# Attention with head mixing and a rational feed-forward layer: the planner spaces bulk transfers evenly during attention

## The chip, the core and the metric

The kernel runs on 1 core of a Trainium2 chip. The metric is the device time of one execution in microseconds. Three runs gave 833.57, 831.95 and 833.22 us; the median is 833.22 us.

## What is computed

The reference, cut to what matters (batch 4, 12 heads, 448 positions, head size 64; the feed-forward layer has 1792 tokens, width 768, inner width 2048):

```
scores = scale * np.matmul(q, k.transpose(0, 1, 3, 2))
scores = np.einsum('bhij,hg->bgij', scores, w_pre)
scores = scores - np.max(scores, axis=-1, keepdims=True)
attn = np.exp(scores)
attn = attn / (np.sum(attn, axis=-1, keepdims=True) + 1e-09)
attn = np.einsum('bhij,hg->bgij', attn, w_post)
x = np.matmul(attn, v)
...
h = x @ w_in
P = a[0] + a[1] * h + a[2] * h2 + a[3] * h3
Q = 1.0 + np.abs(b[0]) * np.abs(h) + np.abs(b[1]) * h2
g = P / (Q + 1e-06)
return (g @ w_out).astype(np.float32)
```

All products are of float32 accuracy; the weights come as 64-bit floats, and the chip splits each into a high and a low 32-bit part.

## The kernel before

**Attention** works on 16 tiles of query rows, four per batch element, of 120 or 88 rows. For each tile six pairs of heads are multiplied on TensorE (`put_qk`, line 482, matmul on line 496, PSUM tile `ps_s`). Each head's scores are copied to SBUF by ACT or DVE (tile `st`), and then a transfer on SP's queue, the **shuffle** (line 512, `d<-st`), lays them out so that heads lie along the partitions. There are twelve shuffles per tile, one per head. The first matmul of the next stage (`put_pre`, line 565, `ps_t` or `ps_u` from `d`) mixes the heads and waits for all twelve shuffles of its tile. A tile is worked on in groups of two blocks of ten rows: mix (L565), maximum (L571, DVE), exponential (L580, ACT), sum and reciprocal, mix again (L640, `ps_a`), transpose (L656, DVE), and, when a tile's groups are through, the product with V (L705, `put_av`, 56 matmuls in the profile for each third). The shuffles of tile T are issued while TensorE works on the groups of tile T - 1. The scores of tile 0 are made ahead of all that.

**Bulk transfers** share SP's queue with the shuffles: loads of Q (L363, 384 KB), K (L375, six parts of 224 KB per batch element from the second on), V (L679, three of 384 KB and one of 192 KB per element), weights (L405, tile `cr`), stores of the attention output (L728, `x_scr`), and, for the first two blocks of weights (`VIA = (0, 1)`), stores of the split weights to DRAM (L449, `w_scr`). Those two blocks are split by ACT, POOL and DVE in between during attention and come back at the end of it (L843).

**The feed-forward part** begins near 346 us and runs 64 units of 18 + 18 matmuls (L879, L969) with the rational function on ACT and DVE in between.

**The order of the work** on each engine is set by the class `Plan`. Every step is an operation with an engine, an assumed duration, operations that it depends on, a due time `at` and an earliest time `since`. `Plan.run` (line 73) walks through planner time: for each engine it takes, among the operations that are ready, the one with the smallest `at`. For SP it also holds `dma_free`, the assumed time at which the transfers issued so far have moved (bytes at 300 GB/s), and lets SP run ahead of it by 3.0 us at most. The result is an order per engine. On the chip each engine follows its order and waits for semaphores; no planner time is left in the program. SP, too, waits at a transfer whose data are not there, and what stands behind it waits with it.

The helper `bulk` (line 356) adds a load or store on SP; the weight loads (line 451) and the stores to `w_scr` (line 470) are added directly, as are the shuffles (line 529).

Of the kernel before, what the change touches and what calls it, by code (L numbers as in the profile page):

```python
# [37 lines left out]
CV = 384  # L38
# [5 lines left out]
class Op:  # L44
    __slots__ = ("eng", "dur", "fn", "deps", "at", "extra", "start", "end", "left", "behind", "since", "n", "on", "pick", "mode", "late")

    def __init__(self, eng, dur, fn, deps, at, extra, since, mode, late):
        self.late = late
        self.since, self.on, self.pick, self.mode = since, None, isinstance(eng, dict), mode
        self.eng, self.dur, self.fn, self.at, self.extra = eng, dur, fn, at, extra  # L50
        self.deps = deps
        self.start = self.end = None


class Plan:
# [8 lines left out]
    def __init__(self):  # L64
        self.ops = []

# [6 lines left out]
    def run(self):  # L73
# [36 lines left out]
        order = []  # L110
        last = None
        while True:
            if "sp" in free:
                free["sp"] = max(free["sp"], dma_free - self.AHEAD)
            best = None
            for e in todo:
# [4 lines left out]
                if todo[e]:  # L121
                    t = free[e]
                elif wait[e]:
                    t = max(free[e], wait[e][0][0])
                else:
                    continue
# [5 lines left out]
            while wait[e] and wait[e][0][0] <= t:  # L132
                _, n, op = heapq.heappop(wait[e])
                if op.on:
                    continue
                heapq.heappush(todo[e], (op.at, n, op))
            op = todo[e][0][2]
            if e == "pe" and op.mode != last:
                more = [x for x in todo[e] if not x[2].on and x[2].mode == last and x[0] <= op.at + self.SLACK]
                if more:  # L140
                    op = min(more)[2]
# [100 lines left out]
def mixed_attention_then_rational_ffn(ctx: ExitStack, tc, q, k, v, w, wmix, mask, a, b2, out):  # L242
# [113 lines left out]
    def bulk(dur, fn, deps, at, nbytes, **more):  # L356

        return add("sp", dur, fn, deps, at=at, extra=dma(nbytes), **more)

# [39 lines left out]
    def put_w(f, c, at, since=0.0, g=None):  # L399
# [50 lines left out]

        ld = add("sp", 0.45, load, [R["cr"].take()], at=at - 5.0, extra=dma(128 * CV * 8), since=max(since, at - 9.0))
        near = lambda i, k: [] if g is None else [posts[min(g + i, len(groups) - 1)][k]]
# [16 lines left out]
        if f in VIA:  # L469
            o8 = add("sp", 0.57, store, [o7], at=at, extra=dma(128 * CV * 8), late=2.0)  # L470
            R["co"].uses[-1].append(o8)
# [583 lines left out]
    for u in range(len(units)):  # L1055
# [3 lines left out]
        put_unit(u)  # L1059

    with tc.manual_schedule():
        for op in plan.run():
# [59 lines left out]
```

## Time and profile before

| what | value |
|---|---|
| median of 3 runs | 833.22 us (831.95 to 833.57) |
| profiled execution, its own time | 835.32 us |
| its span, first to last instruction | 833.5 us |
| mean granted TensorE clock | 0.994 of full speed |
| busy: PE, DVE, ACT, POOL | 804.6, 698.1, 503.1, 217.4 us |

Busy time is the time in which an engine has an instruction under way; the rest of the span it waits. PE is TensorE, SP the engine that issues most transfers. The profiled execution lies 2.1 us above the median of the runs.

### The profile page before, as it was taken

Reading aid. Unit: us, or ns where it says so; the run is one execution under the profiler, and the core shown is the slowest. Engines: PE = TensorE matmul, PEld = TensorE weight load, DVE = VectorE, ACT = ScalarE, POOL = GpSimd, SP = SyncE. Lnnn points to the kernel's source line nnn. Section 1 sums busy time; section 2 is a strip of 40 time slices with the busy share of each in tenths; the row PEclk is TensorE's granted clock in tenths of the full one; section 3 lists DMA queues with packets and bytes.
Section 4 is the critical chain, followed back from the end, with each engine's and each line's share of the span. In section 5 each row is a group of like instructions: output and inputs, shape, how many; then the busy total and the mean of one; then the engine's idle time right before and its main releaser. Section 6 shows DMA issues by size and latency. Waiting matters only on the chain.

```text
span 833.5 us, 23249 instructions
## 1 busy us (share of the span) xinstructions
PE 804.6 (97%) x9360; PEld 598.0 (72%) x9360; DVE 698.1 (84%) x1262; ACT 503.1 (60%) x1094; POOL 217.4 (26%) x388
## 2 busy tenths in 40 slices
PE   6899999998999899999999999999999999999997
PEld 1244445554455455588999999999999999999997
DVE  5677778787887878898999999999889999877775
ACT  2456656655564556567776676676666676745632
POOL 2224434342442334612211112122222222200000
PEclk9999999999999999999999999999999999999999
DMA  6676788678766855965731364664476635466314
GB/s 207 214 218 201 209 267 275 187 213 274 231 189 199 260 176 170 328 189 209 255 124 61 101 240 117 212 142 85 102 231 179 166 91 107 90 226 232 124 53 155
DMA packets 69724, 152.31 MB, mean 183 GB/s; under 512 B 12432, under 2 KB 50160, under 8 KB 68464
## 3 DMA queue, kind: packets, MB, share of 16 engines
q1 hardware_dynamic: 65560, 138.84, 51.0%
q0 software_dynamic: 3456, 11.01, 8.3%
q8 instruction: 74, 1.21, 0.6%
q10 hardware_dynamic: 600, 0.97, 0.4%
q14 instruction: 34, 0.28, 0.1%
HBM read 75.92 MB, written 36.18 MB: 134 GB/s over the span
## 4 chain that ended last, share of the span: by engine, by line
PE 60%; DVE 3%; ACT 1%; DMA 1%; issue 1%; POOL 0%; ACTq 0%; POOLq 0%
PE ps_s L879 27%; PE ps_u L969 9%; PE ps_a L969 9%; PE ps_t L969 9%; PE ps_a L640 2%; PE ps_s L496 1%; PE ps_u L705 1%; PE ps_t L565 1%; PE ps_u L565 1%; DMA w<-w_scr 1%; PE ps_t L705 0%; ACT e L580 0%; DVE cg L424 0%; DVE nm L571 0%; DVE cm L430 0%
## 5 line engine op out<-in xcount | busy, mean ns | idle before, releaser
L656 DVE STREAM_TRANSPOSE aa<-ps_a 128x448 f32<-128x448 f32 (+1 forms) x184 | 107.5, 617 | 12.7 <-PE ps_a L640 12.1
L879 PE MATMUL ps_s<-xs,w 128*128 128x448 f32 x504 | 107.5, 366 | 0.2 <-DVE m L908 0.2
L879 PE MATMUL ps_s<-d,w 128*128 128x448 f32 x504 | 107.6, 367 | 0.0
L496 PE MATMUL ps_s<-kk,q 64*64 64x448 f32 x720 | 94.8, 553 | 8.3 <-DMA kk<-in_k 5.1
L236 ACT COPY st<-ps_s 120x448 f32<-120x448 f32 (+1 forms) x116 | 58.2, 533 | 71.5 <-PE ps_s L496 34.2
L446 POOL TENSOR_TENSOR w<-cm,w 128x384 fp32r<-128x384 f32 x48 | 56.2, 1171 | 171.6 <-ACT w L236 133.7
L879 PEld LDWEIGHTS ps_s<-xs,w 128*128 128x128 f32 x504 | 94.4, 188 | 8.9 <-DVE m L908 0.6
L879 PEld LDWEIGHTS ps_s<-d,w 128*128 128x128 f32 x504 | 94.3, 188 | 8.9 <-issue 0.5
L640 PEld LDWEIGHTS ps_a<-e,krs 64*32 64x32 f32 x2880 | 45.1, 106 | 75.4 <-issue 29.1
L600 POOL TENSOR_SCALAR krs<-kpost,rr 128x64 f32<-128x64 f32 x180 | 80.7, 462 | 70.4 <-DVE rr L591 48.8
L640 PE MATMUL ps_a<-e,krs 64*32 64x224 f32 x2880 | 94.1, 358 | 1.6 <-DVE aa L656 0.9
L892 ACT ACTIVATE m<-ps_s,a_sb 128x448 f32<-128x448 f32 x64 | 46.3, 724 | 68.9 <-PE ps_s L879 68.5
L969 PE MATMUL ps_t<-g,w 128*128 128x448 f32 x336 | 84.0, 366 | 1.2 <-ACT g L236 1.0
L969 PE MATMUL ps_a<-g,w 128*128 128x448 f32 x336 | 84.1, 366 | 0.0
L969 PE MATMUL ps_u<-g,w 128*128 128x448 f32 x336 | 83.9, 366 | 0.0
L580 ACT ACTIVATE e<-ps_t,nm 128x448 f32<-128x448 f32 x92 | 57.7, 634 | 25.5 <-DVE nm L571 21.4
L580 ACT ACTIVATE e<-ps_u,nm 128x448 f32<-128x448 f32 x88 | 55.3, 635 | 28.9 <-DVE nm L571 24.1
L969 PEld LDWEIGHTS ps_t<-g,w 128*128 128x128 f32 x336 | 63.0, 188 | 7.0 <-ACT g L236 1.2
L969 PEld LDWEIGHTS ps_u<-g,w 128*128 128x128 f32 x336 | 63.1, 188 | 5.4
L969 PEld LDWEIGHTS ps_a<-g,w 128*128 128x128 f32 x336 | 63.1, 188 | 5.4
L496 PEld LDWEIGHTS ps_s<-kk,q 64*64 64x64 f32 x720 | 29.7, 135 | 50.4 <-issue 21.5
L587 POOL TENSOR_SCALAR sm<-sm 128x2 f32<-128x2 f32 (+1 forms) x92 | 20.9, 227 | 140.1 <-ACT e L580 138.3
(90 smaller groups left out, 1468.2 us busy)
## 6 DMA issues: line engine op xcount, KB each, us to landing
d<-st SPq DMA_DIRECT2D x144, 210.0 KB
cr<-in_w SPq DMA_DIRECT2D x64, 384.0 KB
d<-x_scr SPq DMA_DIRECT2D x5, 2688.0 KB
xs<-x_scr SPq DMA_DIRECT2D x4, 2688.0 KB
o_scr<-o POOLq DMA_DIRECT2D x24, 448.0 KB, 6.0
d<-st SPq DMA_DIRECT2D x42, 157.5 KB
x_scr<-xs SPq DMA_DIRECT2D x12, 540.0 KB
q<-in_q SPq DMA_DIRECT2D x16, 384.0 KB
```

Source lines behind the costliest of these rows:

```text
L236: eng.copy(o, i)
L446: eng.tensor_sub(t[:, 1, :], box["m"].bitcast(F32), t[:, 0, :].bitcast(F32))
L496: nc.tensor.matmul(box["s"][hh][i0:i1, 0:S], lhsT=Q[T][d, pr, i0:i1], rhs=K[b][d, pr, :], start=True, stop=True)
L565: nc.tensor.matmul(box[r if nt == 2 else 0]["t"][64 * c:64 * c + 64, 0:S], lhsT=kpre[p], rhs=Dt[T][p, kb + c if nt == 2 else kb, :], start ...
L580: nc.scalar.activation(e, box[r]["t"][:, 0:S], AF.Exp, bias=box[0]["nm"][:, r:r + 1], accum_out=box[0]["sm"][:, r:r + 1])
L587: nc.gpsimd.tensor_scalar_add(sm, sm, 1e-9)
L600: eng.tensor_scalar_mul(box[r]["kr"], kpost, rr)
L640: nc.tensor.matmul(banks[c]["p"][q_:q_ + BT, JH * r:JH * (r + 1)], lhsT=box[r]["kr"][p, m_, :], rhs=box[r]["e"][p, JH * jh:JH * (jh + 1)], ...
L656: nc.vector.transpose(o, src)
L879: nc.tensor.matmul(h[:, 0:S], lhsT=W[fi][:, wi, kk * 128:(kk + 1) * 128], rhs=x[:, kk // 3, xj, kk % 3, :], start=(n == 0), stop=(n == 3 * ...
L892: nc.scalar.activation(new("m"), box["h"], AF.Identity, scale=a_sb[:, 3:4], bias=a_sb[:, 2:3])
L969: nc.tensor.matmul(O[key][:, 0:S], lhsT=W[fi][:, wi, DM + m * 128:DM + (m + 1) * 128], rhs=box["g"][:, gi, :], start=(f == 0 and n == 0), ...
```

## The change

`Plan` gets a stretch of planner time, from `tau[2]` to `END1 - 24.0` (23.3 to 335.3 us), and a gap of 2.4 us. Every operation added through `bulk` is marked with `gap`. When SP takes a marked operation in that stretch, no other marked one may be taken before 2.4 us later; marked operations that are ready meanwhile are put aside, and SP takes an unmarked one (a shuffle above all) or waits. The weight loads and the stores to `w_scr` are now added through `bulk`, so that they are marked too. Which blocks of weights go through DRAM stays (`VIA = (0, 1)`).

```diff
@@ class Plan
     def __init__(self):
-        self.ops = []
+        self.ops, self.spaced, self.gap = [], (0.0, 0.0), 0.0
...
+        held = 0.0
+        aside = []
         while True:
             if "sp" in free:
                 free["sp"] = max(free["sp"], dma_free - self.AHEAD)
+                if aside and held <= free["sp"]:
+                    for x in aside:
+                        heapq.heappush(todo["sp"], x)
+                    aside = []
...
                 elif wait[e]:
                     t = max(free[e], wait[e][0][0])
+                    if e == "sp" and aside and held < t:
+                        t = held
+                elif e == "sp" and aside:
+                    t = held
...
+            if e == "sp":
+                if aside and held <= t:
+                    for x in aside:
+                        heapq.heappush(todo[e], x)
+                    aside = []
+                while todo[e] and (todo[e][0][2].on or todo[e][0][2].gap and t < held):
+                    x = heapq.heappop(todo[e])
+                    if not x[2].on:
+                        aside.append(x)
+                if not todo[e]:
+                    continue
             op = todo[e][0][2]
+            if op.gap and self.spaced[0] <= t < self.spaced[1]:
+                held = t + self.gap
...
@@ def bulk(dur, fn, deps, at, nbytes, **more):
-        return add("sp", dur, fn, deps, at=at, extra=dma(nbytes), **more)
+        op = add("sp", dur, fn, deps, at=at, extra=dma(nbytes), **more)
+        op.gap = True
+        return op
...
@@ def put_w
-        ld = add("sp", 0.45, load, [R["cr"].take()], at=at - 5.0, extra=dma(128 * CV * 8), since=max(since, at - 9.0))
+        ld = bulk(0.45, load, [R["cr"].take()], at=at - 5.0, nbytes=128 * CV * 8, since=max(since, at - 9.0))
...
-            o8 = add("sp", 0.57, store, [o7], at=at, extra=dma(128 * CV * 8), late=2.0)
+            o8 = bulk(0.57, store, [o7], at=at, nbytes=128 * CV * 8, late=2.0)
...
+    plan.spaced, plan.gap = (tau[2], END1 - 24.0), 2.4
     with tc.manual_schedule():
```

What this does to the order is seen on SP. The rows below are SP's order of issue, without times; line numbers of the changed kernel lie 25 higher (L363 is L388, L679 is L704, L512 is L537, L375 is L400, L405 is L430). `x2` is two in a row.

**Tile 2, whose twelve shuffles are the `d<-st` rows here.** SP before:

```order
L363 DMA q<-in_q 128x768
L679 DMA vv<-in_v 128x768 x3
L512 DMA d<-st 10x12x448 x2
L679 DMA vv<-in_v 128x384
L512 DMA d<-st 10x12x448 x4
L363 DMA q<-in_q 128x768
L512 DMA d<-st 10x12x448 x2
L375 DMA kk<-in_k 128x448
```

SP with the change, the same place:

```order
L388 DMA q<-in_q 128x768
L704 DMA vv<-in_v 128x768 x2
L537 DMA d<-st 10x12x448 x2
L704 DMA vv<-in_v 128x768
L537 DMA d<-st 10x12x448 x2
L704 DMA vv<-in_v 128x384
L537 DMA d<-st 10x12x448 x2
L388 DMA q<-in_q 128x768
L537 DMA d<-st 10x12x448 x2
L400 DMA kk<-in_k 128x448
```

The third V load moved from ahead of the first shuffle to behind the second, and the half load from behind the second to behind the fourth.

**From the end of tile 7 to the end of tile 8.** SP before, beginning with the last two shuffles of tile 7:

```order
L512 DMA d<-st 10x12x448 x2
L363 DMA q<-in_q 128x768
L679 DMA vv<-in_v 128x768
L512 DMA d<-st 10x12x448 x6
L679 DMA vv<-in_v 128x768
L512 DMA d<-st 10x12x448 x6
L679 DMA vv<-in_v 128x384
```

SP with the change; the q load behind the first row here is the one that stood there before:

```order
L537 DMA d<-st 10x9x448 x2
L704 DMA vv<-in_v 128x768
L388 DMA q<-in_q 128x768
L704 DMA vv<-in_v 128x768
L537 DMA d<-st 10x12x448 x6
L704 DMA vv<-in_v 128x768
L537 DMA d<-st 10x12x448 x4
L704 DMA vv<-in_v 128x384
L537 DMA d<-st 10x12x448 x2
```

A V load that stood between tile 7's shuffles now follows them, and the half load moved ahead of tile 8's last two shuffles.

**Tile 15, the last one.** SP before, from the last shuffles of tile 14 (`10x12x448`) on:

```order
L512 DMA d<-st 10x9x448 x6
L405 DMA cr<-in_w 128x768
L512 DMA d<-st 10x9x448 x2
L405 DMA cr<-in_w 128x768
L512 DMA d<-st 10x9x448 x4
L449 DMA w_scr_119<-co 256x1x384
```

SP with the change:

```order
L537 DMA d<-st 10x12x448 x4
L430 DMA cr<-in_w 128x768
L537 DMA d<-st 10x9x448 x4
L430 DMA cr<-in_w 128x768
L537 DMA d<-st 10x9x448 x4
L430 DMA cr<-in_w 128x768
L537 DMA d<-st 10x9x448 x4
L474 DMA w_scr_119<-co 256x1x384
```

A weight load moved from tile 14 to the front of tile 15, and the next one from behind shuffle 6 to behind shuffle 4. In tile 10 two of three K loads moved from between the shuffles to behind the last. On PE and POOL the order is the same row for row; on ACT and DVE it is the same in attention but for one copy of scores in tile 14 that goes from DVE to ACT, and one pair of neighbours on ACT, and in the feed-forward part some neighbours change places.

## Rows read from the trace of the kernel before

**Rows 1.** The page's busy times: us (share of the span), number of instructions.

```profile
PE 804.6 (97%) x9360; PEld 598.0 (72%) x9360; DVE 698.1 (84%) x1262; ACT 503.1 (60%) x1094; POOL 217.4 (26%) x388
```

**Rows 2.** Table by stage: stretch, length, busy of each engine, PE clock, DMA share, GB/s.

```profile
24.00:346.00 322.00, 307.07 (x6579) 153.21 (x6575) 257.84 (x473) 191.62 (x517) 122.74 (x291) 0.99 0.73 224
400.00:829.00 429.00, 429.00 (x2107) 394.94 (x2105) 381.54 (x686) 269.09 (x496) 75.74 (x71) 1.00 0.51 148
```

**Rows 3.** PE's waits, 24 to 346 us: total us, times, longest.

```profile
PE ps_u L705 <- issue: 2.3, 2, 1.7
...
PE ps_a L640 <- DVE rr L591: 0.4, 1, 0.4
```

**Rows 4.** PE's timeline: start, us, instruction, count, [idle before <- what ended it].

```profile
35.79 0.98 PE L565 MATMUL ps_t<-d,kpre 64*64 64x448 f32 x8 [0.79 <-DMA vv<-in_v]
...
59.22 0.98 PE L565 MATMUL ps_u<-d,kpre 64*64 64x448 f32 x8 [1.10 <-DMA kk<-in_k]
...
184.87 1.12 PE L565 MATMUL ps_t<-d,kpre 64*64 64x448 f32 x8
...
203.59 0.30 PE L705 MATMUL ps_u<-aa,vv 64*64 64x90 f32 x3 [1.70 <-issue]
...
207.34 0.98 PE L565 MATMUL ps_u<-d,kpre 64*64 64x448 f32 x8 [0.95 <-DMA q<-in_q]
...
229.05 0.98 PE L565 MATMUL ps_t<-d,kpre 64*64 64x448 f32 x8 [0.22 <-DMA kk<-in_k]
...
289.32 0.98 PE L565 MATMUL ps_u<-d,kpre 64*64 64x448 f32 x8 [1.93 <-ACT xs L236]
...
334.88 0.98 PE L565 MATMUL ps_t<-d,kpre 64*64 64x448 f32 x8 [0.81 <-PE ps_a L640]
```

**Rows 5.** SP's timeline at tiles 1 and 2, transfers issued in a row merged.

```profile
29.25 1.61 SPq L512 DMA_DIRECT2D d<-st  x2
...
31.45 1.57 SPq L679 DMA_DIRECT2D vv<-in_v  x3
38.12 1.65 SPq L512 DMA_DIRECT2D d<-st  x2
...
50.17 1.67 SPq L512 DMA_DIRECT2D d<-st  x2
```

**Rows 6.** SP's timeline: the last shuffles of tiles 9 and 10.

```profile
195.92 4.80 SPq L512 DMA_DIRECT2D d<-st  x4
...
219.22 3.35 SPq L512 DMA_DIRECT2D d<-st  x4
```

**Rows 7.** SP's timeline: the last six shuffles of tile 8.

```profile
171.26 6.01 SPq L512 DMA_DIRECT2D d<-st  x6
```

**Rows 8.** SP's timeline at tile 15.

```profile
323.19 0.49 SPq L405 DMA_DIRECT2D cr<-in_w  x1
324.80 3.72 SPq L512 DMA_DIRECT2D d<-st  x4
```

**Rows 9.** Transfers by line: count, KB each.

```profile
vv<-in_v SPq DMA_DIRECT2D x12, 384.0 KB
kk<-in_k SPq DMA_DIRECT2D x18, 224.0 KB
```

**Rows 10.** Table by stretches of 4 us, columns as in rows 2.

```profile
52.00:56.00 4.00, 3.41 (x104) 2.24 (x100) 2.19 (x4) 1.58 (x5) 1.09 (x3) 1.00 0.92 223
...
200.00:204.00 4.00, 2.30 (x91) 1.67 (x72) 1.91 (x3) 1.34 (x4) 0.48 (x2) 1.00 0.74 217
204.00:208.00 4.00, 3.05 (x56) 1.31 (x52) 2.94 (x6) 2.97 (x9) 0.86 (x2) 1.00 0.99 322
...
288.00:292.00 4.00, 2.68 (x32) 0.95 (x40) 1.93 (x4) 1.45 (x6) 1.09 (x3) 0.83 1.02 320
292.00:296.00 4.00, 4.00 (x72) 1.40 (x56) 2.66 (x4) 2.37 (x7) 0.22 (x1) 0.74 0.68 216
...
316.00:320.00 4.00, 4.00 (x87) 1.62 (x72) 3.72 (x9) 3.33 (x10) 1.94 (x5) 1.00 0.40 123
```

More of the change, by code (lines that the diff above doesn't have):

```diff
@@ L44 @@
 class Op:
-    __slots__ = ("eng", "dur", "fn", "deps", "at", "extra", "start", "end", "left", "behind", "since", "n", "on", "pick", "mode", "late")
+    __slots__ = ("eng", "dur", "fn", "deps", "at", "extra", "start", "end", "left", "behind", "since", "n", "on", "pick", "mode", "late", "gap")
     def __init__(self, eng, dur, fn, deps, at, extra, since, mode, late):
-        self.late = late
+        self.late, self.gap = late, False
         self.since, self.on, self.pick, self.mode = since, None, isinstance(eng, dict), mode
```

## The prediction

> **What bounds the kernel now.** I first read the page's busy times: TensorE (PE) works for 97% of the span and the next engine, DVE, for 84% [rows 1]. The table by stage then splits the span [rows 2]. From 400 to 829 us, the feed-forward part, PE is busy for 429.00 of 429.00 us; nothing that only moves transfers in the attention part can take time from there. From 24 to 346 us, the attention part, PE is busy for 307.07 of 322.00 us: it stands for 14.9 us, and the DMA engines are busy for 0.73 of the time. So the question is what happens to these 14.9 us. The view of PE's waits in that stretch lists them by what ended them; two of its rows are shown, 2.3 us that ended with "issue" (no event that the profile shows) and 0.4 us for DVE [rows 3].
>
> The timeline of PE shows where the long waits lie [rows 4]. The matmul group of L565 (the one that reads the shuffled scores d) needs all twelve shuffles of its tile of rows. The waits of 0.79, 1.10, 0.95, 0.22 and 0.81 us at 35.79, 59.22, 207.34, 229.05 and 334.88 us stand before the first L565 group of tiles 1, 2, 9, 10 and 15. The last one is put down to PE itself, which had long been done, so I count it to the shuffles too. The queue of SP shows the shuffles and the bulk transfers in the order of issue [rows 5 to 8]. From the end of the issue of a tile's last shuffle to the first L565 of that tile it takes 35.79 - 30.86 = 4.9 us in tile 1, with almost no bulk transfers among its shuffles, but 59.22 - 51.84 = 7.4 us in tile 2, 207.34 - 200.72 = 6.6 in tile 9, 229.05 - 222.57 = 6.5 in tile 10 and 334.88 - 328.52 = 6.4 in tile 15. A shuffle thus waits behind bulk transfers that were issued before it.
>
> **What the change does.** It gives SP no clock: the 2.4 us exist in the planner's time alone, and the program gets another order of the same transfers. On PE the order stays the same row for row; in attention ACT takes one copy of scores that DVE had, in tile 14. So the cost of the change is what the new order puts ahead of the last shuffle of a tile, or takes from there. Evenness by itself earns nothing if the same bytes stand ahead of the twelfth shuffle; a gain needs a transfer moved behind it, or into a time when the engines are idle, and a loss is the reverse. The DMA engines are never free of work for long in attention, but SP waits before a tile's first shuffle, and a transfer issued in that pause moves for nothing.
>
> The Trainium skill bears on this, in "DMA: Bandwidth & Descriptors", section "Queues, rings and completion order": a transfer of SP's queue is split over up to 16 rings, and each ring is consumed in order. By that rule no shuffle overtakes a bulk transfer issued earlier, and the sum is the one below; if shuffles could overtake, every term below would be 0. No run here shows the rings themselves.
>
> **Tile 2, a loss.** Before, three V loads are issued at 31.45 to 33.02 us (31.45 + 1.57), and SP then stands until 38.12 [rows 5]. Now the third V load is issued behind the first two shuffles and the half load two shuffles later. The third load is 384 KB [rows 9], or 393 kB, and it is new among the work ahead of shuffles 3 to 12. Its price: at the 322 GB/s of the fullest stretch, 204 to 208 us [rows 10], it takes 1.22 us; at the 223 GB/s of 52 to 56 us, 1.76 us; if the engines have room for it, 0. I take 1.2, since between 52 and 56 us the engines are busy for 0.92 of the time and the tile already waits: the wait at 59.22 grows from 1.10 to 2.3 us. Ends: 0 and 1.8. The half load also arrives later, and the first product with V (L705, tile 0) reads it; a wait there would delay PE inside a stretch whose end is set by the shuffles at 59.22, so I cost it at nothing. Should the shuffles come early, this is what is late next.
>
> **Tiles 8 and 9, a small loss.** A V load of tile 7 and a half load of tile 9 come into tile 8's stretch: 384 KB [rows 9] and half of that, 590 kB, 1.8 us at 322 GB/s. Tile 8 has no wait now: 184.87 - 177.27 = 7.6 us lie between its last shuffle and its first L565, where the late tile 9 needed 6.6 us [rows 4, 7]. So about 1.0 us is covered; 0 to 0.8 us is not. I take 0.3, as the whole load is issued in SP's pause ahead of tile 8's first shuffle. Tile 9 itself keeps its order of sizes: an x store after each second or fourth shuffle, three in all, before and now; its wait of 0.95 stays, with ends -0.6 (the half load gone, 197 kB at 322 GB/s) and 0.
>
> **Tile 10, a small gain.** Two K loads of 224 KB [rows 9], 459 kB together and 1.4 us at 322 GB/s, go behind the last shuffle. The wait is only 0.22 us [rows 4], so the gain is 0.2, with ends 0 and 0.2. PE is next bound by its own order there. The K loads fall into tile 11's stretch, which has no wait among those of rows 4, so I cost that at 0.
>
> **Tile 15, a gain.** The weight loads (cr) that stood after shuffles 6 and 8 (the second issued at 323.19 us [rows 8]) now stand after shuffles 4 and 8, and a third one, from tile 14, stands ahead of the first shuffle, in SP's pause. Between 316 and 320 us the DMA share is 0.40 [rows 10], so the load after shuffle 4 moves with room, and the queue behind shuffle 8 gets shorter by up to its 1.2 us. The wait of 0.81 can go entirely or stay. I take -0.5. What is late next is DVE, for which PE waits 0.4 us behind that [rows 3].
>
> **What else moves.** Tile 7 gains a K load and loses a V load, which is larger [rows 9]: 0. The stores to w_scr wait for POOL and hold the shuffles behind them on SP; they move back by a shuffle or two, when POOL, whose order stays, is further: 0.
>
> **What is not touched.** The 1.93 us at 289.32 are a wait for an ACT cast; its order and its inputs stay. The 1.70 us at 203.59 are an "issue" wait in the midst of an L705 group, with no transfer of SP's queue named. The copy that moves from DVE to ACT in tile 14 has no PE wait near it: 0.
>
> **Sum:** 1.2 + 0.3 - 0.2 - 0.5 = +0.8 us. The profiled execution took 835.32 us, of which 833.5 are the span; it would take 836.1. It lies 2.1 us above the median of the runs, 833.22, so the forecast for the median is 834.0 us. A measurement of this kernel tells about 0.2% (1.7 us) from no change; my sum is within that.
>
> **Rivals.** (1) *Even spacing shortens the queue for all tiles.* Then the waits of tiles 2, 9, 10 and 15 vanish: 1.10 + 0.95 + 0.22 + 0.81 = 3.1 us, giving 830.1 us. For it: the DMA share swings between 0.40 and 1.02 in stretches of 4 us [rows 10], and the change levels just that. Against it: in tiles 2 and 9 no bytes leave the stretch ahead of the last shuffle, and transfers still touch where the planner thought a pause was (a V, a q and a V load in a row before tile 8). The Trainium skill would favour it: "DMA: Bandwidth & Descriptors", section "Latency and other measured facts", gives memory access as 0.2 us on average and 2 us at high load, so a smoother load lowers the fixed part of each transfer. By that rule an estimate of up to 2 - 0.2 = 1.8 us per transfer could go, more than any of the four waits, and the time would again be 830.1. No row here separates that part. Chance 0.25.
>
> (2) *The longer wait at tile 2 lets TensorE's clock fall.* After the wait of 1.93 us at 289.32 the granted clock was 0.83 and then 0.74 of full speed in two stretches of 4 us [rows 4, 10], a fall to the lower of its two levels (1.2 instead of 2.4 GHz) for part of each, which cost 4 x 0.17 + 4 x 0.26 = 1.7 us. If the wait at 59.22 grows past 1.93 us, the same can happen near 60 us: 834.0 + 1.7 = 835.7 us, slower. For it: my 2.3 us is longer than that wait. Against it: between 200 and 208 us PE waited 1.70 and 0.95 us, and both windows there show the full clock [rows 4, 10]. With the upper ends of tile 2 (+0.6) and tile 8 (+0.5) it gives 836.8. Chance 0.2; the upper ends of the costs without the clock add 0.13 on the same side.
>
> (3) *The change does nothing on the chip*, since only the order moves and SP's waits for the copies set the pace: 833.2 us. Chance 0.12, on the same side of the line as my forecast, which has 0.30 by itself.
>
> **How the numbers follow.** Faster by over 0.2%: rival 1, 0.25. Within 0.2%: forecast and rival 3, 0.42. Slower: rival 2 and the upper ends, 0.33. The range goes from rival 1 (830.1, cut to 830.4) to rival 2 with its ends (836.8), and I leave 1 in 10 outside on either side. The likeliest time is 834.0; by itself my sum runs from 833.2 - 0.2 - 0.8 - 0.6 = 831.6 (all lower ends) to 833.2 + 1.8 + 0.8 = 835.8.
>
> **What would show it.** Right: the wait before tile 2's first L565 (now near 60 us) is about 2.3 us, tile 10's is gone, tile 15's is shorter, and PE stays without a gap from 400 us on. The wait at 289.32 reappears, later by what tile 2 lost. Wrong: tile 2's wait stays at 1.1 or less, so the V load moved in idle time; tile 8 waits for over 0.8 us; a new stretch with a granted clock under 0.9 appears near 60 us; or the waits of tiles 9 and 10 both go, which would speak for rival 1.

## The result and the profile after

The changed kernel takes 837.52 us (median of 16 runs, 835.75 to 842.74), the kernel before, run beside it, 833.40 us (16 runs, 831.66 to 837.42). The ratio is 1.0053, 95% interval 1.0033 to 1.0074: slower by 0.53%, about 4.4 us of 833.4. The prediction was 834.0 us with a range of 830.4 to 836.8; the median lies 0.7 us above it. The profiled execution took 840.42 us with a span of 838.6, so it is 2.9 us above the median, and before it was 835.32 with 833.5, 1.9 us above its own. The pair of traces thus shows 5.1 us, a little more than the runs do. Of these, 0.85 us are there at the first score group of tile 1 (36.64 against 35.79 us), whose shuffles stand as before: the scatter of the start is in both traces.

The lines that answer to [rows 1, 2]: the page's busy times, and the table by stage (the attention part now ends 4 us later, so the stretches are 24 to 350 and 400 to 834 us).

```profile
PE 802.4 (96%) x9360; PEld 596.8 (71%) x9360; DVE 701.2 (84%) x1263; ACT 501.2 (60%) x1093; POOL 216.0 (26%) x388
```

```profile
24.00:350.00 326.00, 305.63 (x6572) 152.00 (x6564) 255.90 (x468) 191.27 (x517) 120.63 (x286) 0.99 0.73 219
400.00:834.00 434.00, 434.00 (x2137) 400.55 (x2136) 390.94 (x700) 271.94 (x504) 75.22 (x72) 1.00 0.51 148
```

The feed-forward part is as before, busy without a gap. In attention PE stands for 326.00 - 305.63 = 20.4 us where it stood for 14.9. The timeline of PE shows the waits, in the form of [rows 4]; L590 is the old L565, and L730 the old L705.

```profile
48.52 0.39 PE L730 MATMUL ps_u<-aa,vv 64*64 64x90 f32 x8 [1.30 <-DMA vv<-in_v]
...
61.94 0.98 PE L590 MATMUL ps_u<-d,kpre 64*64 64x448 f32 x8 [1.61 <-DVE aa L681]
...
107.21 0.98 PE L590 MATMUL ps_u<-d,kpre 64*64 64x448 f32 x8 [2.07 <-DVE rr L616]
...
128.81 0.98 PE L590 MATMUL ps_t<-d,kpre 64*64 64x448 f32 x8 [1.08 <-DVE aa L681]
...
213.33 1.77 PE L590 MATMUL ps_u<-d,kpre 64*64 64x448 f32 x8 [2.83 <-DMA kk<-in_k]
...
296.17 0.29 PE L730 MATMUL ps_t<-aa,vv 64*64 64x90 f32 x1 [1.59 <-issue]
...
340.25 0.98 PE L590 MATMUL ps_t<-d,kpre 64*64 64x448 f32 x8
```

Tile 2 (61.94) waits 1.61 us in place of 1.10, with a new wait of 1.30 us for V ahead of it. Tile 4 (107.21) waits 2.07 us and tile 5 (128.81) 1.08; before, neither had a wait. Tile 9 (213.33) waits 2.83 us in place of 0.95. Tile 15 (340.25) does not wait, as the forecast allowed. With tile 9's wait the clock falls, which the same table by stretches of 4 us as [rows 10] shows:

```profile
208.00:212.00 4.00, 2.50 (x48) 0.85 (x44) 3.01 (x6) 2.67 (x9) 0.99 (x4) 1.00 0.77 250
212.00:216.00 4.00, 2.67 (x16) 0.90 (x16) 0.84 (x1) 0.32 (x1) 1.69 (x2) 0.59 0.69 200
```

The group at 213.33 takes 1.77 us instead of 0.98, and the granted clock of 212 to 216 us is 0.59. The like stretch of the kernel before stood behind its wait at 289.32 [rows 4, 10]; near that place PE now waits 1.59 us, at another line (296.17), and the clock stays full. So each of the two traces has one such stretch between 30 and 350 us.

### The profile page after: what moved, and what is told of

Same layout as the page of the kernel before. It is cut to its first block, busy times and chain, and to the rows that moved or that the text cites. A ratio compares the mean times of both kernels' runs of the same rounds, so it can differ in the third digit from the quotient of the medians.

```text
span 838.6 us, 23248 instructions
## 1 busy us (share of the span) xinstructions
PE 802.4 (96%) x9360; PEld 596.8 (71%) x9360; DVE 701.2 (84%) x1263; ACT 501.2 (60%) x1093; POOL 216.0 (26%) x388
## 4 chain that ended last, share of the span: by engine, by line
PE 80%; DMA 7%; DVE 6%; ACT 3%; issue 2%; SPq 1%; POOL 0%; ACTq 0%; POOLq 0%; DVEq 0%
PE ps_s L904 27%; PE ps_u L994 9%; PE ps_a L994 9%; PE ps_t L994 9%; PE ps_s L521 7%; PE ps_a L665 6%; PE ps_u L590 4%; DMA d<-st 3%; PE ps_t L590 3%; PE ps_u L730 3%; PE ps_t L730 3%; ACT e L605 2%; DVE nm L596 2%; DMA kk<-in_k 1%; DMA vv<-in_v 1%
## 5 line engine op out<-in xcount | busy, mean ns | idle before, releaser
L605 ACT ACTIVATE e<-ps_t,nm 128x448 f32<-128x448 f32 x92 | 57.7, 634 | 23.1 <-DVE nm L596 19.1
L596 DVE TENSOR_REDUCE nm<-ps_u 128x2 f32<-128x896 f32 (+1 forms) x45 | 47.4, 1054 | 12.6 <-PE ps_u L590 11.0
```

The source lines that it names most:

```text
L596: nc.vector.tensor_reduce(out=nm[:, 0:nt], in_=box[0]["both"][:, 0:nt, 0:S], axis=AX.X, op=ALU.max, negate=True)
L605: nc.scalar.activation(e, box[r]["t"][:, 0:S], AF.Exp, bias=box[0]["nm"][:, r:r + 1], accum_out=box[0]["sm"][:, r:r + 1])
```

## The experiments

Each time is given as a ratio to the kernel before, run on the same chip between the runs of the experiment (its median was 833.9 to 835.3 us in these sessions), with the 95% interval. Single runs of one kernel scatter with a standard deviation of 2 to 3 us, so one experiment tells about 1.5 to 2 us from nothing. Each also left one profile; with those of before and after these are 20, and together with all the runs they tell more than single ratios, as the end of this section shows. "Stretch" is the time from one tile's first shuffle issue to the landing of its last shuffle.

**The spacing in part of the program.** Three kernels set the window of the spacing and one the ring of copied scores:

```diff
-    plan.spaced, plan.gap = (tau[2], END1 - 24.0), 2.4
+    plan.spaced, plan.gap = (tau[2], tau[first[3]]), 2.4            # e1
+    plan.spaced, plan.gap = (tau[first[5]], END1 - 24.0), 2.4       # e2
+    plan.spaced, plan.gap = (tau[first[3]], tau[first[5]]), 2.4     # e4
```

```diff
-    open_pools(right, "right", (("st", 6), ("q", 3), ("k", 2)))
+    open_pools(right, "right", (("st", 8), ("q", 3), ("k", 2)))     # e3
```

Tiles 2 and 3 (e1). 

> Even spacing only in the planner's tiles 2 and 3: their transfers stand as in the changed kernel, those of tiles 8 to 10, 13 and 14 nearly as before, and in tile 4 the one difference from before is that the third V load stands behind eight shuffles, not ten. Theory (the loss comes in two places, tile 2 with about 1.9 us and tile 4 with about 3.0 us, each from a longer queue behind which the last shuffles land): about 833.4 + 1.9 = 835.3 us if tile 4's loss comes from its weight block, 837 to 838 if it comes from the third V load alone. Rival (all of the loss starts in tile 2, and tile 4 only follows from being late): 837.5 us, with tile 4's wait of about 2 us there again. Rival (the loss is the startup's scatter): 833.4 us.

Measured: 1.0020 (0.9996 to 1.0044). Tile 4's wait is there (1.50 us) and its stretch is 24.55 us, though only its third V load had moved within it: the weight block is not the cause. The time, 835.1 us by this ratio with an upper end of 837.1, is low for the 837 to 838 us expected in that case.

From tile 5 on (e2). 

> Even spacing only from the planner's tile 5 on: tiles 2 to 5 stand as before, 10 to 15 as in the changed kernel, 6 to 9 nearly so. Theory: the two losses of tiles 2 and 4 are gone and tile 15's gain of 0.8 us stays, against a longer wait of about 1 us before tile 9: 833 us, within 0.2% of before. Rival (every evenly filled tile is late by a little): half of the loss or more stays, 835.5 us or above.

Measured: 1.0019 (0.9995 to 1.0043), between the two. Tile 4's stretch is 21.4 us, as before.

Eight buffers (e3). 

> The changed kernel, order unchanged, with eight buffers for copied scores in place of six. Theory (in tile 4 the late landings hold the copies on ACT and DVE, because a copy needs the buffer of the shuffle six back, and the exponentials stand behind those copies): the 3.32 us that ACT waits at 97 us for a shuffle's landing go, and PE's wait of 1.16 us near 98.8 with them; the wait of 2.07 us before tile 4's first L590 stays, since that one is for the landing itself: about 836.4 us. Rival (the ring of six is the whole loss): 833.5 us. Rival (the ring does nothing, the transfers alone set the time): 837.5 us.

Measured: 1.0042 (1.0011 to 1.0074). The ring is not the whole loss. ACT's longest wait for a shuffle's landing falls from 3.3 to 1.2 us (the view of ACT's waits, total, times, longest):

```profile
ACT st L259 <- DMA d<-st: 3.7, 3, 1.2
```

PE's wait of 1.16 us near 98.8 us goes with it, as the theory said, and the time comes back as a longer wait at the landing (PE's timeline of the same run):

```profile
107.72 0.98 PE L590 MATMUL ps_u<-d,kpre 64*64 64x448 f32 x8 [2.40 <-DMA d<-st]
```

So the copies that stand on ACT are a sign of late landings, not what makes them late.

Tiles 3 and 4 (e4). 

> Even spacing only in the planner's tiles 3 and 4, order of the other engines as before: tiles 2 and 3 as before, in tile 4 the weight block moves from behind two shuffles to behind four and the second V load from four to six, the third V load stays behind ten; tiles 5 to 7 are changed, 8 to 15 as before. Theory (what counts is how much stands in the queue ahead of the last shuffles): tile 4 loses 1 to 2 us, 834.4 to 835.4 us. Rival (tile 4's loss comes only on top of tile 2's): 833.4 us. Rival (moving the weight block by itself is the 3.0 us): 836.4 us.

Measured: 1.0025 (1.0000 to 1.0049), tile 4's stretch 23.5 us, its wait 1.66 us.

**Single transfers moved.** From here on a kernel takes the planner's order (gap 0.0 is the order of before, 2.4 that of the change) and puts SP's i-th transfer behind its j-th:

```diff
+        order = plan.run()
+        sp = [op for op in order if op.on == "sp"]
+        for i, j in MOVES:
+            order.remove(sp[i])
+            order.insert(order.index(sp[j]) + 1, sp[i])
-        for op in plan.run():
+        for op in order:
```

Tile 4 alone (e5): gap 0.0, and

```diff
+MOVES = (68, 73), (78, 75)
```

> The kernel before with two transfers moved: in tile 4 the weight block goes from behind the second shuffle to behind the sixth, and the third V load from behind the tenth to behind the eighth. All else as before. Theory (the same bytes take longer when bulk transfers alternate with pairs of shuffles, since the packets of both are then slower): from tile 4's first shuffle issue to the landing of its last one about 24 us, where the kernel before and the run with spacing from tile 5 on took 21.3 and 21.4; PE waits about 1.5 to 2 us before tile 4's first L590 and about 1 us in the groups ahead of it; time 833.4 + 2.5 = 836 us. Rival (tile 4's loss is a consequence of starting late after tile 2): 21.4 us and no wait, 833.4 us.

Measured: 1.0016 (0.9989 to 1.0043), stretch 21.76 us, wait 0.62 us. The time allows the theory and the rival; the stretch, at 21.76 us in place of 24, speaks against the theory, and e15 below, with the same tile 4, has 21.81. Alternating the same transfers with pairs of shuffles does not make tile 4 late.

All but tile 4 (e6): gap 2.4, and

```diff
+MOVES = (73, 67), (76, 78), (82, 83)
```

> The changed kernel with tile 4's transfers put back to where they stood before (weight block behind the second shuffle, third V load behind the tenth, the next q load behind tile 5's first shuffle). Theory: tile 4's stretch is 21.4 us again, without the wait of 2 us; of the 4.1 us lost about 2.5 come back: ratio near 1.002, 835 us. Rival (tile 4 is slow because of what tile 2 and 3 pushed back): the stretch stays at 23.5 us or above, 837.5 us.

Measured: 1.0031 (1.0005 to 1.0057), stretch 21.09 us, no wait at tile 4. The time again allows both; the stretch speaks for the theory. Since e5 excludes the weight block and the V load, the third move is left: the q load that the change issues right behind tile 4's last shuffle. What SP issues at that place, after and before:

```profile
93.71 4.61 SPq L537 DMA_DIRECT2D d<-st  x4
98.37 0.48 SPq L704 DMA_DIRECT2D vv<-in_v  x1
99.23 0.33 SPq L388 DMA_DIRECT2D q<-in_q  x1
```

```profile
93.36 1.63 SPq L512 DMA_DIRECT2D d<-st  x2
95.04 0.53 SPq L679 DMA_DIRECT2D vv<-in_v  x1
101.32 0.78 SPq L512 DMA_DIRECT2D d<-st  x1
102.15 0.48 SPq L363 DMA_DIRECT2D q<-in_q  x1
```

And what the engines moved within tile 4's stretch (the view of the transfers; before, after, e5, e6):

```profile
DMA packets 2284, 4.41 MB, mean 207 GB/s; under 512 B 200, under 2 KB 1768, under 8 KB 2280
```

```profile
DMA packets 2456, 4.85 MB, mean 199 GB/s; under 512 B 213, under 2 KB 1819, under 8 KB 2452
```

```profile
DMA packets 2283, 4.41 MB, mean 203 GB/s; under 512 B 199, under 2 KB 1767, under 8 KB 2279
```

```profile
DMA packets 2284, 4.41 MB, mean 209 GB/s; under 512 B 200, under 2 KB 1768, under 8 KB 2280
```

In the changed kernel 0.44 MB more moved before the last shuffle had landed. A q load is 0.39 MB, 128 packets of 3 KB. Of packets between 2 and 8 KB the changed kernel has 2452 - 1819 = 633, and the other three have 512: 121 more, nearly the whole q load, 0.37 MB. The rest is from the first shuffles of tile 5. At 199 GB/s 0.44 MB take 2.2 of the 3.06 us by which the stretch grew (24.35 to 21.29). Four of the 20 profiles have that q load ahead of tile 5's first shuffle (after, e1, e3, e10): stretches 24.4, 24.6, 23.5 and 25.4 us. Of the other sixteen, fifteen have 21.1 to 22.9, and e4 has 23.5, which stays unexplained. Moving the q load by itself was not tried, so it is found by elimination and by its packets.

Tile 2 alone (e7): gap 0.0, and

```diff
+MOVES = (27, 29), (30, 32)
```

> The kernel before with two transfers moved in tile 2: the third V load behind the second shuffle, the half V load behind the fourth, as in the changed kernel; all else as before. Theory (the third load's bytes are new among the work ahead of the last shuffle, 1.2 us by the prediction): from tile 2's first shuffle issue to its last landing 22.6 us, against 20.7 to 22.3 in three runs with the order of before, and a wait of over 1 us for V near 48 us: 834.6 us. Rival (nothing, the startup's scatter makes tile 2's wait): 833.4 us.

Measured: 1.0028 (1.0006 to 1.0049), which excludes the rival's 1.000; tile 2's stretch is 22.2 us. The V wait is there, and with it the clock falls (PE's timeline, then the table by stretches of 4 us):

```profile
50.78 0.47 PE L730 MATMUL ps_u<-aa,vv 64*64 64x90 f32 x8 [2.02 <-DMA vv<-in_v]
```

```profile
48.00:52.00 4.00, 1.98 (x56) 1.31 (x52) 1.08 (x3) 0.60 (x2) 1.86 (x5) 0.87 0.87 248
52.00:56.00 4.00, 4.00 (x56) 1.40 (x50) 2.25 (x3) 1.28 (x3) 0.00 (x0) 0.71 0.60 201
```

All eight profiles with the V loads in this order wait 0.94 to 2.02 us for V between 46 and 51 us; none of the other twelve does.

Bulk transfers out of the way (e8): gap 0.0, and

```diff
+MOVES = (38, 43), (41, 38), (155, 152), (250, 267), (274, 271)
```

> The kernel before with bulk transfers moved out of the way of last shuffles: both K loads of tile 2 behind its twelfth shuffle, the half V load of tile 9 into tile 8, the weight blocks of tiles 14 and 15 as in the changed kernel (one ahead of the first shuffle, one behind the fourth). Theory (a tile is late by what stands ahead of its last shuffle): the waits of 1.10, 0.95 and 0.81 us before tiles 2, 9 and 15 go, 833.4 - 2.5 = 831 us. Rival (the next thing is late right behind each wait): 833 us or more.

Measured: 0.9990 (0.9965 to 1.0016), no gain that can be told, though the theory's 0.997 is not excluded either. In its profile tile 2 waits 0.87 us where the trace of before had 1.10, and there are new waits of 0.87 us at 76.80 and of 0.86 before tile 4, which speaks for the rival: what is next is late too.

Tile 9 alone (e9), gap 0.0; all but tile 9's stores (e10), gap 2.4 (the shuffles move, so that no store goes ahead of what fills it); all but tiles 2, 4 and 9 (e11), gap 2.4; the half V load alone (e12), gap 0.0:

```diff
+MOVES = (155, 152), (161, 163), (164, 166)                               # e9
+MOVES = (161, 163), (162, 161), (164, 166), (165, 164)                   # e10
+MOVES = (29, 26), (32, 28), (73, 67), (76, 78), (82, 83), (161, 163), (162, 161), (164, 166), (165, 164)  # e11
+MOVES = (155, 152),                                                      # e12
```

> The kernel before with tile 9 as in the changed kernel: its half V load goes into tile 8, its first store of x from behind the second shuffle to behind the fourth, its second from behind the fourth to behind the sixth. All else as before. Theory (SP fills its own pause behind the second shuffle with the first store of x; moved out of it, the store is issued where SP has no pause, and issues that follow a store of x take 1.1 to 2.0 us instead of 0.8): SP issues tile 9's twelve shuffles in 18.6 to 19.1 us instead of 16.3 to 16.8; from tile 8's first L590 to tile 10's 45 us, against 42.1 to 43.1 in three runs with the old order; time 833.4 + 2 = 835.4 us. Rival (the half V load that leaves tile 9 pays for it): 833.4 us or less.

Measured: 1.0030 (1.0005 to 1.0055); the twelve shuffles are issued in 19.1 us, tile 8's first L590 to tile 10's takes 45.4 us. Here is why, in SP's queue at tile 9: the kernel before, then the changed one.

```profile
183.24 1.66 SPq L512 DMA_DIRECT2D d<-st  x2
184.95 0.49 SPq L405 DMA_DIRECT2D cr<-in_w  x1
185.67 0.39 SPq L728 DMA_DIRECT2D x_scr<-xs  x1
187.23 1.65 SPq L512 DMA_DIRECT2D d<-st  x2
188.94 0.48 SPq L728 DMA_DIRECT2D x_scr<-xs  x1
190.49 3.99 SPq L512 DMA_DIRECT2D d<-st  x4
194.53 1.29 SPq L728 DMA_DIRECT2D x_scr<-xs  x1
```

```profile
188.75 1.67 SPq L537 DMA_DIRECT2D d<-st  x2
190.47 0.49 SPq L430 DMA_DIRECT2D cr<-in_w  x1
192.74 1.63 SPq L537 DMA_DIRECT2D d<-st  x2
194.43 0.50 SPq L753 DMA_DIRECT2D x_scr<-xs  x1
196.00 2.40 SPq L537 DMA_DIRECT2D d<-st  x2
198.45 0.49 SPq L753 DMA_DIRECT2D x_scr<-xs  x1
199.03 2.40 SPq L537 DMA_DIRECT2D d<-st  x2
201.49 1.97 SPq L753 DMA_DIRECT2D x_scr<-xs  x1
203.55 5.05 SPq L537 DMA_DIRECT2D d<-st  x4
```

Before, the first store of x fills SP's pause between 185.44 and 187.23. Now SP stands empty from 190.96 to 192.74, and the stores come where it has none. Two shuffles then take 2.40 us to issue, not 1.65, and the third store 1.97. The twelve need 208.60 - 188.75 = 19.85 us, before 17.48. In the six profiles with this order of stores (after, e2, e3, e6, e9, e15) it is 18.2 to 19.9 us, in the other fourteen 16.8 to 18.5.

> The changed kernel with tile 9's two stores of x put back to behind the second and the fourth shuffle. Theory: tile 9's shuffles are issued in 16.3 us, tile 8's first L590 to tile 10's takes 42 to 43 us, the wait of 2.1 to 2.8 us before tile 9 goes; about 2 us come back: ratio 1.003, 835.5 us. Rival (tile 9 is late because the tiles before it are): 837.5 us with that wait still there.

Measured: 1.0059 (1.0037 to 1.0080, six runs), above the theory's 1.003. The mechanism is there in part: the twelve are issued in 18.5 us, less than the 19.85 of the changed kernel but not the 16.3 expected; tile 8 to tile 10 takes 42.6, and tile 9's wait is

```profile
214.87 0.98 PE L590 MATMUL ps_u<-d,kpre 64*64 64x448 f32 x8 [0.42 <-DMA x_scr<-xs]
```

But the time did not come back; this profile has a wait of 3.52 us at tile 4, with a half-clock stretch that costs 3.4 us.

> The changed kernel with tiles 2 and 4 and the stores of x of tile 9 put back; tiles 3, 6 to 8 and 10 to 15 as changed. Theory (the loss is those three places, each alone): nothing of the loss is left, 833 to 833.5 us, ratio 0.998 to 1.001. Rival (spacing itself costs a little in every tile): ratio 1.002 or more, 835 us.

Measured: 1.0033 (1.0011 to 1.0055). The theory's value is outside; the rival's is inside.

> The kernel before with one transfer moved: tile 9's half V load goes into tile 8, behind its tenth shuffle (the one part of the change that took bytes from ahead of a late tile's shuffles). Theory: tile 8's first L565 to tile 10's falls from 42.1 to 43.1 us to 41.8 us, as in the two runs that had this place, 833.4 - 0.8 = 832.6 us. Rival (tile 8 pays for it): 833.4 us or above.

Measured: 1.0021 (0.9995 to 1.0047); tile 9 does not wait, but the time did not fall.

**Where else (e13 to e18)**, gap 0.0 in all:

```diff
+M68 = (103, 105), (102, 108), (106, 112), (109, 115), (110, 117), (113, 119), (121, 126), (123, 128), (124, 130), (131, 133), (134, 136), (137, 139), (155, 152)
+M1012 = (178, 180), (176, 183), (181, 187), (184, 181), (189, 191), (185, 193), (177, 195), (188, 177), (197, 202), (198, 204), (199, 206), (200, 209), (207, 212), (210, 214)
+M1415 = (258, 261), (259, 263), (250, 267), (274, 271)
+MOVES = M68                                                              # e13
+MOVES = M1012 + M1415                                                    # e14
+MOVES = (27, 29), (30, 32), (68, 73), (78, 75), (155, 152), (161, 163), (164, 166)  # e15
+MOVES = M1012                                                            # e16
+MOVES = M1415                                                            # e17
+MOVES = ((27, 29), (30, 32)) + M1012 + M1415                             # e18
```

> The kernel before with tiles 6 to 8 as in the changed kernel (bulk transfers one by one behind each pair of shuffles; the half V load of tile 9 goes into tile 8). All else as before. Theory (the loss is tiles 2, 4 and 9, and elsewhere the twelfth shuffle has slack of about 1 us or more): 833.9 us, ratio 0.998 to 1.001. Rival (what was left when tiles 2, 4 and 9 were put back lies here): ratio 1.002 to 1.003, 836 us, with waits before tiles 6 to 9.

Measured: 0.9999 (0.9982 to 1.0015), the theory's value.

> The kernel before with tiles 10 to 15 as in the changed kernel: here the prediction had gains, 0.2 us before tile 10 and 0.5 before tile 15. Theory now (these waits are not there in most runs with the old order, so nothing can be gained): 833.9 us, ratio 0.999 to 1.001. The prediction: 833.2 us. Rival (what was left when tiles 2, 4 and 9 were put back lies here): ratio 1.002 to 1.003.

Measured: 1.0019 (0.9996 to 1.0042). No gain; whether there is a loss, this one does not tell.

> The kernel before with tiles 2, 4 and 9 as in the changed kernel, all else as before. Theory (these three are the loss): ratio 1.005, 838 us, as for the whole change; tile 1's first L590 to tile 2's about 25.5 us against 23.4 to 24.1 with the old order, tile 8's to tile 10's about 45 against 42 to 43. Rival (half of the loss lies elsewhere): ratio 1.0025, 836 us.

Measured: 1.0018 (0.9991 to 1.0045); tile 1 to tile 2 took 25.3 us, tile 8 to tile 10 only 43.4. The theory's 1.005 is outside, the rival's 1.0025 inside. Its tile 4 has no q load behind its last shuffle and a stretch of 21.8 us.

> The kernel before with tiles 10 to 12 as in the changed kernel (two K loads go behind tile 10's last shuffle into tile 11, a q load from tile 11 into tile 12). The prediction: 0.2 us faster. Theory now (tile 11 is late by the K loads moved into it, as the wait of 0.51 us for a q load before tile 11 in the run with tiles 10 to 15 says): ratio 1.001 to 1.002. Rival: 1.000, and what tiles 10 to 15 cost lies in 14 and 15.

Measured: 1.0016 (0.9996 to 1.0035), which allows theory and rival.

> The kernel before with tiles 14 and 15 as in the changed kernel (a weight block of tile 14 goes ahead of tile 15's first shuffle, one of tile 15 from behind its sixth shuffle to behind its fourth; in tile 14 stores of x move two and four shuffles back). The prediction: 0.5 us faster. Theory now (the wait of 0.81 us before tile 15 is a rare one, so there is nothing to gain): ratio 0.999 to 1.001. Rival (the stores of x moved back in tile 14 hold SP): 1.002.

Measured: 1.0010 (0.9988 to 1.0033), which allows both too.

> The kernel before with tile 2 and tiles 10 to 15 as in the changed kernel, tiles 4, 6 to 9 as before. Theory (the loss is tile 2's V loads and tiles 10 to 15): ratio 1.004 to 1.005. Rival (tiles 4 and 9 hold half of it, and 10 to 15 nothing): 1.0025.

Measured: 1.0029 (1.0007 to 1.0050), the same as tile 2 alone (1.0028): tiles 10 to 15 add nothing here that can be told.

**All 20 profiles together.** PE's timeline gives the time from one tile's first score group to another's in each profile. I took off half the length of each half-clock stretch within it, and averaged over the profiles whose order in that stretch is that of before or that of the change (a third order is left out). The profiles differ in other places too, so the averages hold if the stretches don't act on each other. The bounds are 95%.

| Stretch | as before (profiles) | as changed | difference |
|---|---|---|---|
| tile 1 to 3, V loads of tile 2 | 45.28 (11) | 46.43 (8) | +1.15 +- 0.6 |
| tile 3 to 4, q load behind tile 4 | 21.92 (16) | 24.30 (4) | +2.4 +- 0.6 |
| tile 3 to 5, the same | 44.70 (16) | 45.15 (4) | +0.45 +- 0.7 |
| tile 5 to 8 | 61.51 (11) | 61.55 (6) | 0.0 +- 0.6 |
| tile 8 to 10, stores of x in tile 9 | 42.97 (14) | 43.89 (6) | +0.9 +- 0.8 |
| tile 10 to 13 | 62.52 (11) | 62.77 (9) | +0.25 +- 0.8 |
| tile 13 to 15 | 40.89 (10) | 41.16 (9) | +0.3 +- 0.5 |

The clock is counted from the runs, each of which lists its span and its mean granted clock: span x (1 - clock) is what the half-clock stretches cost. It is 6.9 +- 0.9 us in the 16 runs of the changed kernel and 5.4 +- 0.3 in the 157 runs of the kernel before from the experiments' sessions (those run beside the changed kernel list no clock), +1.5 +- 0.9; the rest of the span is 829.9 +- 1.3 against 827.7 +- 0.3, +2.1 +- 1.4. Where in the span the 1.5 us lie, a mean does not tell. In the pair of traces the attention part has one half-clock stretch of the same length in each, and the start, which the change doesn't touch, costs 5.1 us after and 3.4 before.

**All runs together.** The runs give the parts in time, too, if the parts simply add up. A least-squares fit to the record's 387 runs (all but those of e8; each session has its own level, and a part counts where the kernel has the changed order there) gives +1.0 +- 0.9 us for tile 2, +0.7 +- 1.3 for the q load behind tile 4, +0.75 +- 0.8 for the stores of x in tile 9, -0.2 +- 0.9 for tiles 6 to 8, and +1.4 +- 0.8 for tiles 10 to 15, in all +3.7 +- 1.0. So tiles 10 to 15, where the stretches show +0.55 +- 0.9, do cost something.

## Why the prediction was wrong

The sign of its sum was right and the size was not: +0.8 us forecast, 4.4 measured. Point by point, with the values of the table and of the fit:

- **Tile 2, +1.2 us:** +1.15 +- 0.6, and +1.0 +- 0.9 in the fit. The step was right: a load of V more among the shuffles, and tile 2's stretch grows from 21.5 to 22.7 us (means of the 11 and 8 profiles). In the pair of traces it is 20.69 and 22.56, and of packets between 2 and 8 KB 382 move in place of 265, 117 more (before, then after):

```profile
DMA packets 2401, 4.28 MB, mean 207 GB/s; under 512 B 211, under 2 KB 2131, under 8 KB 2396
```

```profile
DMA packets 2555, 4.69 MB, mean 208 GB/s; under 512 B 228, under 2 KB 2167, under 8 KB 2549
```

  The wait of 2.3 us that the prediction named as its sign did not come. Before tile 2 PE waits 1.2 us on average in the old order (0 to 2.06) and 1.3 in the new (0 to 1.84), because the loss is taken ahead of it, in the wait for V that the prediction costed "at nothing" and named as late next. That the size came out so close is in part luck: it rests on 322 GB/s, called the fullest stretch, which 336 to 340 us with 425 exceeds, while tile 2's stretch itself ran at 208.
- **Tile 4, nothing:** the prediction has no term for it. The table has +2.4 us at tile 4, of which 0.45 +- 0.7 is left at tile 5, where the other order waits in most profiles; the fit has +0.7 +- 1.3. The step that failed: "a transfer issued in that pause moves for nothing", and with it the test of what stands ahead of the twelfth shuffle. The pause behind a tile's last shuffle is idle for SP, not for the engines: tile 4's last shuffle lands 7.1 us after its issue in the trace of before and 9.4 in that of after, and a q load issued behind it took its bytes out of that time. The bytes are shown, the q load alone was not run, and what it costs in the end is not clear of nothing.
- **Tile 9, "keeps its order of sizes", 0 with ends of -0.6 and 0:** +0.9 +- 0.8, in the fit +0.75 +- 0.8. The store of x that filled a pause of SP was moved out of it. I had compared places in the list of shuffles and not the time SP stands at each; [rows 6] showed four shuffles that took 4.80 us to issue, where two take 1.65 in tile 2 [rows 5], and I did not ask why.
- **Tiles 10 and 15, -0.7 us:** nothing was gained because nothing was there. The waits of 0.22 and 0.81 us [rows 4] belong to one execution. Eight further profiles have tile 15 in the old order: seven wait 0.05 us before it and one 0.55 (e12). Ten further ones have tile 10 in the old order: eight don't wait there, one waits 0.29 (e15), and one 2.37 (e9, behind its late tile 9). Tile 10 did not get quicker either. Two K loads went behind its last shuffle, though only one of them had stood between the shuffles, the other ahead of the first; and the q load that stood ahead of the first came among them, which the prediction did not see (SP before, then after):

```profile
203.08 1.25 SPq L363 DMA_DIRECT2D q<-in_q  x1
206.13 1.65 SPq L512 DMA_DIRECT2D d<-st  x2
```

```profile
217.12 1.63 SPq L537 DMA_DIRECT2D d<-st  x2
218.80 0.49 SPq L388 DMA_DIRECT2D q<-in_q  x1
219.61 1.63 SPq L537 DMA_DIRECT2D d<-st  x2
```

  Over the profiles (11 in the old order, 9 in the new) tile 10's stretch grows by 1.3 +- 1.1 us and tile 11's, into which a q load, a weight block and two K loads came from the pause ahead of it, by 1.3 +- 0.8. That this is the loss of tiles 10 to 15 in the fit was not tried.
- **Rival 2, a longer wait lets the clock fall, chance 0.2:** the clock costs 1.5 +- 0.9 us more on average, about the rival's price. Its place is not shown: tile 2's wait grew past 1.93 us in none of the eight profiles with the new order, in e7 the clock falls with the V wait ahead of it, and in the changed kernel's profile with tile 9's wait. Of the kernels that keep the q load behind tile 4, e3 and e10 have the highest cost of the clock in their runs, 7.4 us, and e6, with tile 4 put back, has 5.2 +- 0.7; but e14, with tile 4 as before, has 6.7 +- 0.8.
- **Rival 1, even spacing shortens the queues:** in no stretch of the table. The 0.2 and 2 us that the prediction took for it stand in the Trainium skill, "DMA: Bandwidth & Descriptors", section "Latency and other measured facts", for access to HBM. A shuffle goes from SBUF to SBUF, so they do not bear on the landings that end the four waits.

With the terms as measured in the profiles the sum is 1.15 + 0.45 + 0.9 = 2.5 us of waits at tiles 2, 4 and 9, and 1.5 of clock: 4.0 us with an uncertainty of about 1.5, where the ratio says 4.4 (2.7 to 6.2). The fit gives 2.5 +- 1.2 for the three places and 1.4 +- 0.8 for tiles 10 to 15. So the failed step is that only the place in the list was compared: what is issued in a pause of SP, and whether a pause is left empty, was counted as free. Against the forecast it made tile 9 cost 0.9 us where tiles 8 and 9 together had 0.3, and tile 4 0.45 where it had nothing; the gains of 0.7 us were read from one execution; and the clock, left to a rival, has the largest part, 1.5.

What stays open: the ratios of single parts don't add up well. With tiles 2, 4 and 9 put back the kernel should be as fast as before and measures 1.0033 (e11), 2.8 us with ends of 0.9 and 4.6; and these three together give 1.0018 (e15), not 1.005. The fit puts 1.4 +- 0.8 us outside the three places, in tiles 10 to 15; its cause was not found, and no version here beats the kernel before.

## What to carry to other kernels

A pause of the issuing queue is a resource of its own: see which transfer fills each pause before and after, and count a transfer issued behind the last one that somebody waits for, as long as that one has not landed. Before you count on removing a wait of less than about 1 us, see it in a second profile: here a second one would have struck out both gains. Where a wait grows to about 2 us, add the chance of a half-clock stretch to its price. And when a transfer leaves a place, ask which other one takes it.

## What the runs showed of the hardware

**Bulk behind a shuffle.** The prediction leaned on the Trainium skill, "DMA: Bandwidth & Descriptors", section "Queues, rings and completion order", that each ring is consumed in order. Order within a ring did not protect the shuffle: 121 of the q load's 128 packets, issued behind it, moved before it had landed. The same page of the Trainium skill, section "Why a DMA increments its semaphore by 16 and not by 1", says that a transfer is spread over the largest number of engines up to 16 that divides the outermost sizes of both sides. By that page, as an estimate, a shuffle (120 rows into 10 strided ones) uses 10 engines and a q load of 128 rows all 16, so part of the q load has rings that no shuffle holds up. The trace agrees on the shuffle: between 91 and 93 us of the kernel before all packets are under 2 KB, those of shuffles, and the queue is busy for 65.5% of 16 engines, or 10.5 of them (the view of the transfers):

```profile
DMA packets 299, 0.49 MB, mean 246 GB/s; under 512 B 25, under 2 KB 299, under 8 KB 299
q1 hardware_dynamic: 299, 0.49, 65.5%
```

Six of 16 engines would account for 48 of the 128 rows, and 121 went ahead. How the others did, and how they slow the shuffle, is not shown: no run here shows the rings themselves.

**Issue time.** A pair of shuffles takes 1.63 to 1.67 us to issue on SP, about 0.76 us each. A row of the timeline can be longer because SP waits between them for a copy: the four at 93.71 us take 4.61 us, and none by itself over 0.78. In tile 9 it is the issues themselves that are longer (SP's view of tile d: shortest, median and longest in ns, at 93, at 196 us after, and at 187 before):

```profile
L537 SPq DMA_DIRECT2D d<-st x4: 755/756/779, 93.7 to 97.6; - x4
L537 SPq DMA_DIRECT2D d<-st x4: 789/1151/1510, 196.0 to 200.3; - x4
L512 SPq DMA_DIRECT2D d<-st x2: 762/778/795, 187.2 to 188.1; - x2
```

There a store of x was outstanding, and a store itself took 1.97 in place of 0.49. That what is outstanding slows SP is my reading of these rows; it was not tried apart.

**The clock.** In the 20 profiles PE has 21 waits of 1.88 us or more between 30 and 350 us. With 13 of them the granted clock falls to half, at a cost of 1.7 us in twelve cases and 3.4 in one (at the wait of 3.52 us); with shorter waits it never does. At the start, ahead of all that the change moves, the half-clock stretch of the 20 profiles costs 1.7 to 6.8 us, which is part of the scatter between runs.
